# Pairing the quarter products of dK and dV in a cached-attention backward kernel

## The chip, the core and the metric

The kernel runs on one core of one Trainium2 chip. The metric is the device time of one execution in microseconds (us). Three executions before the change took 1729.28, 1730.04 and 1733.95 us, so the median is 1730.04 us. A separate execution was profiled; its own time is given with the profile below.

## The reference

The program computes one decoder block for two sequences with one new token each, and the gradient of every input. The block is a layer norm modulated by a conditioning vector, attention of 32 heads over a cache of 8192 keys and values per head, and a gated feed-forward layer. The parts that carry the memory traffic are these:

```python
k_cache, v_cache : (2, 32, 8192, 128) bf16        # B, H, Sk, Dh
scores = einsum('bhqd,bhkd->bhqk', q, k_cache) * 128 ** -0.5
p      = softmax(scores)
o      = einsum('bhqk,bhkd->bhqd', p, v_cache)    # then @ wo, residual, layer norm, SwiGLU
_out, _vjp = jax.vjp(f, A_x, A_k_cache, A_v_cache, A_wq, A_wo, B_w1, B_w3, B_w2, c, w_mod)
return (_out, *_vjp(grad_out))
```

There is one query per head, so the gradients of the two caches are outer products. For one head, with p the softmax weights, do the gradient of o, and dp = v_cache · do: dV[k, :] = p[k] · do, and dK[k, :] = p[k] · (dp[k] − Σ p·dp) · q · 128 ** -0.5. Each of dK and dV is as large as a cache, 2 MB per head. The program therefore reads K once and V up to twice, and writes dK and dV once, for 2 × 32 = 64 heads.

## The kernel before, in words

**Tiling.** A head's 8192 keys are spread over 128 partitions, 64 keys each (`KK`). All large tiles are halves of a head: 128 partitions by 32 keys by 128 values in bf16, 1 MB, 8 KB per partition. They come from one pool of 21 buffers called `half` (`NHALF`). K halves, V halves, the output halves of dK and dV, the large weights and some other things all use this pool.

**Jobs.** A head has two jobs. Job A (lines 390 to 572, `job_a`) is the forward part: it loads K and V, transposes K on TensorE in 8 groups (`a_t`), forms the scores, the maximum, the exponentials, scales K by the exponentials in four quarter products on VectorE (`a_scale`, L468), and contracts with V (`a_m`, L483). Job C (lines 1133 to 1239) is the backward part: it loads V again, transposes it in 8 groups (`c_t`), forms dp (`c_s`, or `c_rows` and `c_cols` for the heads in the set `crow`), turns that into ds (`c_ds`, L1212), and writes dV and dK. Before job C's first slot, `c_spread` puts the two row vectors of the head, called `DOr` (for dV) and `Qr` (for dK), on all partitions.

**Quarter products.** `outer` (L1184) makes one quarter of dV or dK: one VectorE product of 128 x 2048 elements (L1191), half of a half tile. It takes a new `half` buffer when the quarter is the first of its half tile, and issues the 1 MB store to memory from GpSimd's queue (L1196) when the quarter is the second. Six slots after the store, the planner counts the buffer as free (`back`) and lets loads that are due go out (`pump`).

**Order.** The whole order of work is written out by hand, as a list of slots. `at(slot, place, f)` puts a piece of work in a slot, and `place` sets the order within a slot: transposes (`PL_T`) come before the maximum (`PL_MAX`), then the K scaling and dV products (`PL_TT`), then ds (`PL_DS`), then dK products (`PL_DK`), then other tasks. Every engine executes its instructions in the order that this list gives. Loads are issued from SyncE's queue in the order of their due slot, as early as the count of free buffers lets `pump` issue them. The real waits on buffers are semaphores.

**Stages.** A job occupies 8 slots of transposes (`NG`) and further slots for what follows. From the code's arithmetic, slots 0 to 319 hold 40 jobs A, one every 8 slots. From slot 320 to 703, 24 jobs A and 24 jobs C alternate, each pair taking 16 slots, with job C on the first 8. From slot 704 on there are 40 jobs C alone, one every 8 slots; the second sequence's feed-forward chain and what leads to its attention gradient are laid beside them in slots 721 to 777. The last job C starts at slot 1016, which the code calls `max(sC)`. Heads 25 to 31 and the last two heads (62 and 63) are not in `crow`; all others are.

**Where the products lie before.** With job C starting at slot s, the four dV quarters (`c_dv`) lie at s, s+2, s+4 and s+6. The four dK quarters (`c_dk`) lie at s+11, s+13, s+15, s+17, or one slot later for heads in `crow`. The ds they need is made at s+10, or s+11 in `crow`.

Of the kernel before, what the change touches and what calls it, by code (L numbers as in the profile page):

```python
# [17 lines left out]
def kernel(  # L18
# [44 lines left out]
    NG = KK // GRP  # L63
    NQ = KK // QK
    LAG = 2
# [119 lines left out]
    def load_v(key, i, hf):  # L185
        t = htile()
        qd.dma_start(t[:], src_of(A_v_cache, i)[:, hf * HK:(hf + 1) * HK, :])
        free["half"] -= 1
        V[(key, hf)] = t
# [138 lines left out]
    def at(slot, place, f):  # L328
        seq[0] += 1
        events.setdefault(slot, []).append((place, seq[0], f))  # L330

    now = [0]
    PL_EXP, PL_T, PL_X, PL_S, PL_B, PL_MAX, PL_TT, PL_M, PL_FREE, PL_EV, PL_DS, PL_DK, PL_TASK = range(13)
# [4 lines left out]
    def want(need, f):  # L338
        seq[0] += 1
        loads.append((need, seq[0], f))  # L340
# [725 lines left out]
    sC = []  # L1066
    s = NG * H
# [10 lines left out]
    s = max(s, TC)  # L1078
# [12 lines left out]
    s = max(s, t1 + 5)  # L1091
# [41 lines left out]
    def c_t(n, g):  # L1133
        if g == 0:
            if n in crow:
                b, h = hb(n)
                nc.gpsimd.tensor_copy(qz[2 + n % 2][:, NSL - 1:NSL], DO_bf[:, b, h:h + 1])
            else:
                DP[n] = head_ps()
        spare = A_END <= now[0] < t1 or now[0] >= max(sC) - 5 * NG  # L1140
        kts[("c", n, g)] = transposes(lambda j: vb_(("c", n), g * GRP + j), g in (2, 6) and not spare)
        if g % HG == HG - 1:
            V.pop((("c", n), g // HG))
            release()
            pump()

    crow = {n for n in range(NHD) if R0 < sC[n] < A_END - NG or t1 < sC[n]}
# [6 lines left out]
    def c_rows(n):  # L1154
        kts[("crow", n)] = rows_out(("c", n))

    def c_cols(n):
        DP[n] = head_ps()
        cols_out(DP[n], kts.pop(("crow", n)))

    def c_s(n, g):
        if n in crow:
            return s_rows(("c", n), n, g, c_bank)
        b, h = hb(n)
        kt = kts.pop(("c", n, g))
        for j in range(GRP):
            cc = g * GRP + j
            nc.tensor.matmul(DP[n][:, cc:cc + 1], kt[:, j, :], DO_bf[:, b, h:h + 1], start=True, stop=True)  # L1168

    def c_spread(n):  # L1170
        b, h = hb(n)
        ps = scr(2 * P) if R0 <= now[0] <= A_END else mtps()[:, 0:2 * P]
        nc.tensor.matmul(ps[:, 0:P], Qr_bf[:, b, h:h + 1].to_broadcast((P, P)), identb[:], start=True, stop=True)
        nc.tensor.matmul(ps[:, P:2 * P], DOr_bf[:, b, h:h + 1].to_broadcast((P, P)), identb[:],
                         start=True, stop=True)
        for k, (nm, bufs) in enumerate((("Qr", 3), ("DOr", 2))):
            t = hw.tile([P, P], BF16, name=nm, tag=nm, bufs=bufs)
            nc.scalar.copy(t[:], ps[:, k * P:(k + 1) * P])
            QD[(n, k)] = t
        e = hw.tile([P, KK, 2], BF16, name="e2", tag="e2", bufs=3)  # L1180
        nc.scalar.copy(e[:], E["t"][:, n % E["n"], :].unsqueeze(2).to_broadcast((P, KK, 2)))
        E2[("c", n)] = e

    def outer(store, dst, n, which, w2, q):  # L1184
        hf, o = divmod(q * QK, HK)
        if o == 0:
            free["half"] -= 1
            store[(n, hf)] = htile()
        t = store[(n, hf)]
        ks = slice(q * QK, (q + 1) * QK)  # L1190
        nc.vector.tensor_tensor(  # L1191
            pair(t[:, o:o + QK, :]),
            QD[(n, which)][:].rearrange("p (a b) -> p a b", b=2).unsqueeze(1).to_broadcast((P, QK, P // 2, 2)),
            w2[:, ks, :].unsqueeze(2).to_broadcast((P, QK, P // 2, 2)), ALU.mult)
        if o + QK == HK:
            sq_.dma_start(src_of(dst, n)[:, hf * HK:(hf + 1) * HK, :], t[:])  # L1196
            store.pop((n, hf))

            def back():
                release()  # L1200
                pump()

            at(now[0] + 6, PL_FREE, back)

    def c_dv(n, q):
        outer(dvt, out_3, n, 1, E2[("c", n)], q)
        if q == NQ - 1:
            QD.pop((n, 1))

    def c_ds(n):  # L1210
        t = hw.tile([P, KK, 2], BF16, name="ds2", tag="ds2", bufs=2)
        nc.vector.scalar_tensor_tensor(t[:], DP.pop(n)[:, 0:KK].unsqueeze(2).to_broadcast((P, KK, 2)),  # L1212
                                       SIG_f[:, n:n + 1], E2.pop(("c", n))[:], ALU.subtract, ALU.mult)
        ds2[n] = t

    def c_dk(n, q):
        outer(dkt, out_2, n, 0, ds2[n], q)
        if q == NQ - 1:
            ds2.pop(n)
            QD.pop((n, 0))  # L1220

    for n in range(NHD):
        s = sC[n]
        for g in range(NG):
            at(s + g, PL_T, lambda n=n, g=g: c_t(n, g))
            at(s + g + LAG, PL_S, lambda n=n, g=g: c_s(n, g))
        at(s - 3, PL_B, lambda n=n: c_spread(n))
        for q in range(NQ):
            at(s + 2 * q, PL_TT, lambda n=n, q=q: c_dv(n, q))
            at(s + NG + LAG + 1 + (n in crow) + 2 * q, PL_DK, lambda n=n, q=q: c_dk(n, q))  # L1230
        x = 1 if n in crow else 0
        if x:
            at(s + NG + LAG, PL_EXP, lambda n=n: c_rows(n))
            at(s + NG + LAG + 1, PL_EXP, lambda n=n: c_cols(n))
        at(s + NG + LAG + x, PL_DS, lambda n=n: c_ds(n))

        for hf in range(2):
            if n not in kept:
                want(s + hf * HG, lambda n=n, hf=hf: load_v(("c", n), n, hf))
# [304 lines left out]
```

## Time and profile before

| Quantity | Value |
|---|---|
| Median of three executions | 1730.04 us |
| Profiled execution, its own time | 1731.2 us |
| Profiled execution, span from first to last instruction | 1729.4 us |
| TensorE matmul busy | 1447.8 us, 84% |
| VectorE (DVE) busy | 1149.6 us, 66% |
| ScalarE (ACT) busy | 1046.1 us, 60% |
| GpSimd (POOL) busy | 344.9 us, 20% |
| Bytes moved | 708.92 MB, mean 410 GB/s |
| Loads on SyncE's queue (q1) | 421.59 MB |
| Stores on GpSimd's queue (q0) | 268.45 MB |
| Granted TensorE clock, mean | 0.828 |

The profile calls the queue of a DMA by the engine that issues it: SP for loads, POOL for stores of dK and dV, ACT for small outputs. The DMA share in a window is the mean busy share of the core's 16 DMA engines; it is summed from packet durations and reads 1.01 when all of them are busy without a gap. A "half" in a row's name is a buffer of the shared pool.

### The profile page before, as it was taken

To read this page: it belongs to the slowest core of one execution; us is meant where nothing else is said; L and a number is where in the kernel's file an instruction comes from. 1 tells how busy PE (TensorE), PEld (TensorE's weight loads), DVE (VectorE), ACT (ScalarE), POOL (GpSimd) and SP (SyncE) were. 2 spreads that over 40 slices of the span, in tenths; PEclk is the share of its full clock that TensorE was granted. 3 is DMA by queue.
4 is the path that set the end of the run, shared out by engine and by line. 5 is a ranking of instruction groups with operands and counts; after the bars stand their busy time and mean duration, and the time that the engine had idled before them with its cause. 6 is when DMAs were issued, how large, how long until landed. Compare 5 with 4: busy or idle time off the path is not lost.

```text
span 1729.4 us, 48571 instructions
## 1 busy us (share of the span) xinstructions
PE 1447.8 (84%) x20883; PEld 1155.6 (67%) x20883; DVE 1149.6 (66%) x1575; ACT 1046.1 (60%) x1536; POOL 344.9 (20%) x726
## 2 busy tenths in 40 slices
PE   5999999989988878887788888975599997797962
PEld 5999998879776666665666666875355565455551
DVE  2666666867877677666667766785586675666554
ACT  4666666646565556555555555697576676566772
POOL 0333333322211111111111112111121111111111
PEclk7999999988999898898888998698765567556586
DMA  9999999999999999999999998999999999999997
GB/s 382 418 418 419 418 419 388 419 387 390 379 412 424 425 425 420 424 418 418 420 419 418 424 419 358 397 416 420 426 411 419 413 410 419 423 420 420 417 420 303
DMA packets 109379, 708.92 MB, mean 410 GB/s; under 512 B 11175, under 2 KB 17683, under 8 KB 27243
## 3 DMA queue, kind: packets, MB, share of 16 engines
q1 hardware_dynamic: 67280, 421.59, 59.4%
q0 software_dynamic: 36864, 268.45, 37.4%
q10 hardware_dynamic: 5019, 15.78, 2.3%
q8 instruction: 163, 2.67, 0.6%
q14 instruction: 53, 0.43, 0.1%
HBM read 421.57 MB, written 284.20 MB: 408 GB/s over the span
## 4 chain that ended last, share of the span: by engine, by line
DMA 45%; PE 35%; DVE 6%; ACT 6%; issue 5%; SPq 1%; POOL 0%; ACTq 0%; POOLq 0%; DVEq 0%
DMA out_dram<-half 24%; DMA half<-in_A_k_cache_dram 16%; PE tp L380 14%; PE m_ps L483 8%; DVE half L1191 4%; DMA out_dram<-stg 3%; ACT kt L385 3%; PE s_ps L442 2%; PE k_ps L505 2%; PE s_ps L433 2%; PE m_ps L413 1%; DMA half<-in_w_mod_dram 1%; PE m_ps L1323 1%; DVE ek L468 1%; PE k_ps L413 1%
## 5 line engine op out<-in xcount | busy, mean ns | idle before, releaser
L385 ACT COPY kt<-tp 128x1024 bf16<-128x1024 bf16 x794 | 796.6, 1017 | 560.0 <-PE tp L380 511.4
L380 PE MATMUL tp<-identb,half 128*128 128x128 bf16 x8192 | 725.3, 243 | 85.8 <-DMA half<-in_A_k_cache_dram 51.2
L380 PEld LDWEIGHTS <-half 128*128 128x128 bf16 x8192 | 579.7, 110 | 212.5 <-issue 149.0
L383 DVE COPY kt<-tp 128x1024 bf16<-128x1024 bf16 x230 | 158.6, 690 | 294.0 <-PE tp L380 291.5
L483 PE MATMUL m_ps<-ek,half 128*128 128x129 bf16 x4096 | 335.6, 225 | 6.9 <-DVE ek L468 3.8
L1196 POOL DMA_DIRECT2D out_dram<-half x256 | 136.2, 532 | 895.2 <-DVE half L1191 734.6
L483 PEld LDWEIGHTS <-half 128*128 128x128 bf16 x4096 | 257.3, 100 | 28.0 <-issue 27.7
L433 PE MATMUL s_ps<-ssel,srow 128*128 128x16 f32 x640 | 98.6, 288 | 49.6 <-ACT srow L420 49.2
L433 PEld LDWEIGHTS s_ps<-ssel,srow 128*128 128x128 f32 x640 | 91.8, 221 | 63.7 <-ACT srow L420 63.4
L442 PE MATMUL s_ps<-qT_bf,kt 128*128 128x1 bf16 x2496 | 107.4, 164 | 0.8 <-DVE lnst L1030 0.4
L442 PEld LDWEIGHTS <-kt 128*128 128x128 bf16 x2496 | 96.6, 97 | 1.3 <-issue 1.0
L1324 ACT CAST stg<-m_ps 128x512 bf16<-128x512 f32 (+2 forms) x124 | 72.8, 588 | 36.0 <-DMA out_dram<-stg 17.6
L1323 PE MATMUL m_ps<-half 2*128 2x512 bf16 (+2 forms) x124 | 70.1, 565 | 12.4 <-DVE d_h_312 L1436 7.3
L505 PE MATMUL k_ps<-half,pz 128*32 128x512 bf16 x1024 | 68.7, 389 | 3.4 <-POOL pz L491 3.2
L454 DVE TENSOR_REDUCE nm<-s_ps 128x1 f32<-128x128 f32 x64 | 18.7, 291 | 36.0 <-PE s_ps L451 35.9
L1168 PE MATMUL s_ps<-DO_bf,kt 128*128 128x1 bf16 x576 | 25.6, 165 | 18.6 <-DVE kt L383 14.5
L505 PEld LDWEIGHTS <-pz 128*32 128x32 bf16 x1024 | 21.6, 97 | 25.1 <-POOL pz L491 5.6
L1168 PEld LDWEIGHTS <-kt 128*128 128x128 bf16 x576 | 24.4, 101 | 19.8 <-DVE kt L383 14.6
L1323 PEld LDWEIGHTS <-half 2*128 2x128 bf16 (+1 forms) x124 | 12.7, 102 | 34.3 <-issue 31.7
L413 PE MATMUL k_ps<-kt,qz_110 128*32 128x512 bf16 x240 | 32.9, 525 | 1.0 <-ACT kt L385 1.0
L413 PE MATMUL k_ps<-kt,qz_109 128*32 128x512 bf16 x240 | 33.3, 535 | 0.0
L1298 ACT CAST half<-m_ps 2x512 bf16<-2x512 f32 (+1 forms) x36 | 20.2, 565 | 20.0 <-PE m_ps L1295 19.4
(899 smaller groups left out, 1996.3 us busy)
## 6 DMA issues: line engine op xcount, KB each, us to landing
out_dram<-half POOLq DMA_DIRECT2D x256, 1024.0 KB, 17.9
half<-in_A_v_cache_dram SPq DMA_DIRECT2D x252, 1024.0 KB, 14.3
half<-in_A_k_cache_dram SPq DMA_DIRECT2D x128, 1024.0 KB, 19.6
out_dram<-stg ACTq DMA_DIRECT2D x22, 512.0 KB, 11.5
half<-in_A_wq_dram SPq DMA_DIRECT2D x8, 1024.0 KB, 13.0
half<-in_A_wo_dram SPq DMA_DIRECT2D x4, 1024.0 KB, 21.6
half<-in_w_mod_dram SPq DMA_DIRECT2D x3, 1024.0 KB, 10.9
half<-in_B_w_dram SPq DMA_DIRECT2D x3, 1024.0 KB
```

What stands on the lines that cost most here:

```text
L380: nc.tensor.transpose(tp[:, j, :], block(j), identb[:])
L383: nc.vector.tensor_copy(kt[:], tp[:])
L385: nc.scalar.copy(kt[:], tp[:])
L413: nc.tensor.matmul(R_ps[key][NR * j:NR * (j + 1), :], w, kt[:, o:o + SW, :], start=(a == 0), stop=(a == NSL - 1))
L433: nc.tensor.matmul(sv[:, c, :], t[:, c * P:(c + 1) * P], ssel[:], start=True, stop=True)
L442: nc.tensor.matmul(S_ps[i][:, cc:cc + 1], kt[:, j, :], qT_bf[:, h, b:b + 1], start=True, stop=True)
L483: nc.tensor.matmul(m[:, 0:P + 1], vb_(i, kk), t[:, kk % QK, 0:P + 1], start=(kk == 0), stop=(kk == KK - 1), skip_group_check=True)
L505: nc.tensor.matmul(kp["ps"][NR * j:NR * (j + 1), :], pz[:, o:o + NR], K[(i, kk // HK)][:, kk % HK:kk % HK + QP, :], start=False, stop=(h = ...
L1191: nc.vector.tensor_tensor(pair(t[:, o:o + QK, :]), QD[(n, which)][:].rearrange("p (a b) -> p a b", b=2).unsqueeze(1).to_broadcast((P, QK, ...
L1196: sq_.dma_start(src_of(dst, n)[:, hf * HK:(hf + 1) * HK, :], t[:])
L1323: nc.tensor.matmul(ps[:lw, 0:rw], rsl(ln, lc, lw, step), rsl(rn, rc, rw), start=True, stop=True)
L1324: nc.scalar.copy(st["t"][:lw, o:o + rw], ps[:lw, 0:rw])
```

## The change

The change moves the quarter products to other slots. Nothing else in the program is edited, and no operation is added or removed. The numbers are: `NG` = 8, `LAG` = 2, `NQ` = 4.

```diff
@@ for n in range(NHD): s = sC[n]
         for q in range(NQ):
-            at(s + 2 * q, PL_TT, lambda n=n, q=q: c_dv(n, q))
-            at(s + NG + LAG + 1 + (n in crow) + 2 * q, PL_DK, lambda n=n, q=q: c_dk(n, q))
+            x, y = 2 + q + q // 2 * 2, NG + LAG + 2 + q + (q // 2 * 2 if s < max(sC) else 0)
+            at(s + x, PL_TT, lambda n=n, q=q: c_dv(n, q))
+            at(s + y, PL_DK, lambda n=n, q=q: c_dk(n, q))
```

The dV quarters now lie at s+2, s+3, s+6 and s+7: the two quarters of one half tile are in neighbouring slots. The dK quarters lie at s+12, s+13, s+16 and s+17 for all heads, in `crow` or not. In the last job they lie at s+12, s+13, s+14 and s+15. The `half` buffer is still taken at the first quarter of a half tile and the store is still issued at the second, so these two now lie one slot apart where they were two slots apart.

## The prediction, made before the changed kernel was run

> **What bounds the kernel now.** I read four views, from coarse to fine. First, the page's 40 slices.
>
> ```profile
> DVE  2666666867877677666667766785586675666554
> DMA  9999999999999999999999998999999999999997
> GB/s 382 418 418 419 418 419 388 419 387 390 379 412 424 425 425 420 424 418 418 420 419 418 424 419 358 397 416 420 426 411 419 413 410 419 423 420 420 417 420 303
> ```
>
> The DMA engines are busy in every slice but slice 25 and the last one. No compute engine comes near that. The change touches only work from slot 320 on, so I asked for windows by stage (columns: window, length, busy time of each engine with its count, granted clock, DMA share, GB/s).
>
> ```profile
> 270.00:480.00 210.00, 196.60 (x3843) 177.80 (x3840) 151.33 (x289) 121.72 (x178) 56.70 (x107) 0.94 0.99 391
> 480.00:1060.00 580.00, 478.21 (x6248) 374.13 (x6248) 402.44 (x479) 323.07 (x491) 101.19 (x276) 0.90 1.01 421
> 1060.00:1095.00 35.00, 28.38 (x480) 24.13 (x477) 29.34 (x36) 19.56 (x32) 8.74 (x16) 0.80 0.84 323
> 1095.00:1712.00 617.00, 492.30 (x5126) 345.58 (x5123) 408.72 (x519) 420.39 (x615) 92.28 (x183) 0.67 1.01 418
> 1712.00:1729.00 17.00, 0.00 (x0) 0.00 (x0) 0.00 (x0) 0.00 (x0) 0.00 (x0) 0.50 0.30 128
> ```
>
> The alternating stage (480 to 1060) and the stage of jobs C alone (1095 to 1712) run with all 16 DMA engines full. The one hole inside the changed part is 1060 to 1095. It lacks (1.01 − 0.84) × 35 = 6 us of DMA work. The last 17 us is the drain: compute ended at about 1706, and the engines finish one after another.
>
> Third, the waits. The first row is GpSimd's store queue, the others SyncE's load queue and VectorE.
>
> ```profile
> POOL out_dram L1196 <- DVE half L1191: 734.6, 161, 20.8
> SPq L187 <- DMA out_dram<-half: 772.6, 100, 21.7
> SPq L181 <- DMA out_dram<-half: 194.6, 45, 5.0
> DVE half L1191 <- DMA out_dram<-half: 111.4, 30, 16.7
> ```
>
> A store waits for its product, a load waits for a store to give its buffer back, and a product may wait for a buffer too. This is a closed loop through the DMA engines. It stays full as long as some issued bytes are still under way. To see the cover, I subtracted from the bytes issued the bytes whose packets had ended, every 0.5 us, from the trace's DMA records (in MB of 1,048,576 bytes). In the alternating stage the mean is about 3 MB and the lowest point of most 40 us stretches lies between 1.2 and 2 MB, 3 us at 0.42 MB per us. In the stage of jobs C alone, from 1140, the mean is mostly 3 to 6 MB with low points of 1.4 MB near 1143 and 1.26 MB near 1253 and else above 2.4 MB. At 1068 it is 0.07 MB: that is the hole.
>
> Fourth, VectorE's order of time at the hole.
>
> ```profile
> 1057.72 1.23 DVE L1191 TENSOR_TENSOR half<-Qr,ds_20501 128x2048 bf16<-128x2048 bf16 x1 [2.40 <-DMA out_dram<-half]
> 1058.86 0.68 DVE L383 COPY kt<-tp 128x1024 bf16<-128x1024 bf16 x1
> 1059.46 1.22 DVE L1191 TENSOR_TENSOR half<-Qr,ds_20501 128x2048 bf16<-128x2048 bf16 x1
> 1060.59 1.22 DVE L1191 TENSOR_TENSOR half<-DOr,e_20552 128x2048 bf16<-128x2048 bf16 x1
> 1064.78 1.22 DVE L1191 TENSOR_TENSOR half<-Qr,ds_20501 128x2048 bf16<-128x2048 bf16 x1 [2.97 <-PE tp L380]
> 1065.93 0.68 DVE L383 COPY kt<-tp 128x1024 bf16<-128x1024 bf16 x1
> 1066.53 1.22 DVE L1191 TENSOR_TENSOR half<-DOr,e_20552 128x2048 bf16<-128x2048 bf16 x1
> 1067.66 1.22 DVE L1191 TENSOR_TENSOR half<-Qr,ds_20501 128x2048 bf16<-128x2048 bf16 x1
> 1068.79 0.22 DVE L446 TENSOR_REDUCE rm<-s_ps 128x1 bf16<-128x64 f32 x1
> ```
>
> Two half tiles are being filled at once here, dK of head 23 (`Qr`) and dV of head 24 (`DOr`). The second half of dK waits until 1064.78 for a buffer that the transposes still read. Its store goes out at 1068.04 and the one of dV at 1069.17, while the DMA engines starve.
>
> **What the Trainium skill says.** "DMA: Bandwidth & Descriptors", section "Issuing engines are not separate DMA queues": transfers from all issuing engines share the same 16 DMA engines. The trace agrees: loads from SP and stores from POOL together give a share of 1.01. Its section "Where 436 GB/s comes from" puts the ceiling at 435 GB/s; the trace holds 421. So nothing is to be had from moving stores about while the share is 1.01. "VectorE: DVE Perf Modes", section "The perf-mode tier table", gives 1224 ns for a bf16 product of 2048 elements; the trace has 1215 to 1225. "SBUF — State Buffer", section "Who interferes with whom": a VectorE instruction with two SBUF inputs contends with a GpSimd instruction that reads SBUF. The trace is compatible: GpSimd's copy at L470 took 1.08 us beside a product at 1070.04, and 0.24 at 1045.26.
>
> **The change part by part.** It removes and adds nothing: 512 products of 1.22 us and 256 stores of 0.53 us on POOL stay. No edit is costed by a new instruction; what counts is where each store lands and what stands behind it.
>
> *Alternating stage, 24 pairs.* In slots after s (mod 16), stores move from 14, 2, 2, 6 to 13, 1 (dK) and 3, 7 (dV). Their order on VectorE, by the places in a slot, becomes: scale, dK0, dK1, kt copy, dK2, dK3, kt copy, dV0, rm, dV1, nm, kt copy, scale, dV2, dV3, scale. I lay this on the cycle at 924 to 946 and the one before. dK1 falls into the 1.15 us that VectorE waits ahead of the kt copy at 929.13, so its store leaves at about 929 in place of 931.25. dK3 follows the kt copy at 932.0 or so, its store about 4 us ahead of 936.39. dV1 now stands behind dV0 and rm, about 1 us later than 935.26. dV3 stands behind one more product in its slot: 921.0 becomes about 922.1. Sum: −2.2 − 4.2 + 1 + 1.1, so the mean store is 1 us earlier. Behind dV2 and dV3 stands the second `a_scale` product, 1.13 us (the start-to-start step) later; the TensorE product L483 waits for it. VectorE has 1.78 us of idle before the next copy in that cycle (923.63), which takes this up, and TensorE waited for L468 only 3.8 us in the whole stage. All this is hidden by the DMA backlog. The thinnest point is just before the dV3 store; 1.2 to 1.4 MB is 3.0 to 3.5 us, the store is 1.1 us later. Cost 0. Without the cover it would cost 24 × 1.1 = 26 us.
>
> *Jobs C alone.* In `crow` heads, two buffers used to be asked for in the same slot (dV0 with dK2, dV2 with dK0), and both stores of a slot pair came together. Now a half begins every second slot and a store leaves every second slot. A buffer is held one slot less: 7 counted slots in place of 8 for each of four halves in 8 slots, so 3.5 in place of 4 are out on average. That is half a buffer more for loads. The 108.7 us that VectorE waits for stores in this stage may shrink. With the share at 1.01, the gain is 0.
>
> *The hole at 1060 to 1095.* With the new slots, dK of head 23 lies at 700, 701, 704, 705 and dV of head 24 begins at 706. dK1 follows dK0 at once, its store about 0.7 us earlier than 1060.97. dK2 comes ahead of dV0 and gets the buffer that dV0 got at 1060.59. dK3 follows, and the store leaves at about 1063.2 in place of 1068.04. dV0 inherits the wait to 1064.78, behind the kt copy: 1065.4 to 1066.6. Then comes rm, at 1066.6 in place of 1068.79. TensorE waits 2.81 us for this rm with its matmul L451, and all of its later transposes stand behind that, as does the load issued at 1073.95, which waits for transposes. So the chain through the hole is 2.2 us shorter. I take −2.2; bounds are 0 (the buffers come free in another order and the hole only moves) and −5.4 (all of it filled).
>
> *Heads 25 to 31 and the start.* dV stores are one slot later (about 1.5 us) and the dK ones are not earlier, while the backlog from 1095 to 1112 falls to 1.0 MB. The first dV store of all (466.15) is one slot later behind a hole at 456 to 468. I take +0.2 in all, bounds 0 and +3.
>
> *The tail.* The last dK quarters lie in consecutive slots, last store at slot 1031 in place of 1034. VectorE already makes them back to back (four in 4.63 us from 1701.46). Their stores then wait for earlier stores, as these two lines show.
>
> ```profile
> 1705.36 0.53 POOL L1196 DMA_DIRECT2D out_dram<-half  x1 [1.93 <-DMA out_dram<-half]
> 1707.81 0.53 POOL L1196 DMA_DIRECT2D out_dram<-half  x1 [1.93 <-DMA out_dram<-half]
> ```
>
> Gain 0: what is left in flight, about 3 MB at 1700, ends when it ends. The spread of the 16 engines at the end (from about 1712 to 1726) can shift by some us with any change of order; I allow ±4.
>
> Sum: 1731.2 (profiled execution: span 1729.4 and 1.8 around it) − 2.2 + 0.2 = 1729.2. The median of the runs is 1.2 below the profiled one, so 1728.0.
>
> **The rivals.** (1) *The hole closes and more.* Stores are evenly spaced, so the next thin spots (0.26 MB at 1086, 1.0 at 1111) fill as well: −5.4 for the hole and up to −2 at the drain, 1730 − 7 = 1723. For it: VectorE's wait at 1061.8 is a result of two open halves. Against it: while the hole lasts, DVE is 29.3 of 35 us busy, so the work there can't shrink much. (2) *The loop starves* in the alternating stage: dV3's store, and the loads that wait for it, come later than the cover. It decides once the store is more than 3 us late at the thinnest point. At 0.4 us of starvation per pair, 24 × 0.4 = +10, 1740. For it: loads in that stage waited 317.8 us for stores. Against it: three of four stores are earlier or within 1 us. (3) *The products are not paired in time*, because VectorE's queue is full and the waits set the order: nothing moves, 1730.
>
> **How the numbers follow.** About 0.3%, 5.2 us, is what this measurement can tell from no change. Small move from the hole, 1728: 0.45. Nothing, 1730: 0.15. Rival 1: 0.20, mostly beyond 0.3%. Rival 2: 0.20. So faster 0.20, same 0.60, slower 0.20. The likeliest cases' own range is 1724 to 1733. The range takes in the hole's bound, 1730 − 5.4 − 4 = 1721 (rounded), and most of rival 2, to 1738.
>
> **What would show it.** The alternating stage and jobs C keep a DMA share of 1.01. Two products of one half run back to back in their rows, and POOL's stores leave about every 3.8 us in the last stage. The share from 1060 to 1095 rises from 0.84 to about 0.9. TensorE's wait for rm of 2.81 us goes. I am wrong if a window between 480 and 1712 other than the hole falls below 0.97, if SP's wait for stores moves to transposes or products, or if the drain grows past 20 us.

## The result and the profile after

The changed kernel takes 1770.41 us (median of 4 runs, 1770.21 to 1772.47), beside 1731.99 us for the kernel before in the same comparison (1729.28 to 1734.5). The ratio is 1.0225, with a 95% interval from 1.0204 to 1.0245: slower, by 38.4 us in the medians. The forecast was 1728.0 us, with a range from 1721 to 1738. The profiled execution took 1770.21 us, its span is 1768.4 us.

The page's slices of the changed kernel show where the time went.

```profile
DVE  2666666858666566576676666778386665657564
DMA  9999999999999999999999999999999999999997
GB/s 383 419 419 418 418 418 389 419 381 393 377 397 398 390 374 408 397 374 406 380 401 407 387 393 381 364 403 421 426 421 420 417 410 418 423 421 418 421 420 305
```

Before, slices 12 to 24 moved 412 to 425 GB/s. Now the same slices, the alternating stage, move 374 to 408. Slices 25 to 27 hold the end of that stage and the change to the next (364 to 403); from slice 28 to slice 39 the rate is back at 410 to 426. The DMA row alone would hide this: it still reads 9 everywhere. The same in windows by stage (columns as before, the last three being granted clock, DMA share and GB/s):

```profile
480.00:1080.00 600.00, 478.89 (x6029) 377.46 (x6027) 392.86 (x463) 315.67 (x476) 108.45 (x268) 0.87 0.99 395
...
1170.00:1752.00 582.00, 476.48 (x4539) 324.62 (x4536) 388.07 (x456) 396.69 (x583) 86.42 (x176) 0.65 1.01 419
1752.00:1768.00 16.00, 0.00 (x0) 0.00 (x0) 0.00 (x0) 0.00 (x0) 0.00 (x0) 0.50 0.26 110
```

The last stage (419 GB/s, before 418) and the drain are as before. The loss lies in the alternating stage. Between the first dV products of successive heads there were 24.95 us on average before, and there are 26.69 now. Over the 23 such steps that makes 23 × 1.74 = 40 us, which covers the whole loss of 38.4 us.

VectorE's waits from 470 to 1060 name what is new (columns: total us, times, longest). First the kernel before, then the changed one.

```profile
DVE kt L383 <- PE tp L380: 128.7, 59, 7.4
...
DVE half L1191 <- DMA out_dram<-half: 2.4, 1, 2.4
```

```profile
DVE half L1191 <- DMA out_dram<-half: 93.4, 22, 5.9
DVE kt L383 <- PE tp L380: 77.1, 50, 3.9
```

In 22 of about 23 steps VectorE now stands still for some 4 us, until a store to memory has read out the buffer that the next product is to write. Before, only one product of this stage waited so. TensorE then waits for VectorE's copies, and the K loads, behind it all, wait for TensorE. In the same window of the kernel before, TensorE's longest wait was for the K loads themselves:

```profile
PE tp L380 <- DMA half<-in_A_k_cache_dram: 49.8, 29, 4.9
```

These are TensorE's and SyncE's rows of the changed kernel:

```profile
PE tp L380 <- DVE kt L383: 63.0, 25, 4.4
```

```profile
SPq L181 <- DMA out_dram<-half: 84.8, 22, 8.5
SPq L181 <- PE m_ps L483: 54.6, 19, 3.5
```

The chain of waits of the changed kernel, followed back in a window of two steps, closes on itself (columns: start us, us, what).

```profile
902.61 10.60 DMA out_dram<-half
...
913.30 0.13 DVE half L1191
...
925.46 0.14 DVE ek L468
925.61 0.99 issue
926.60 2.37 DVE half L1191 x2
928.96 0.29 issue
929.25 9.82 DMA out_dram<-half
```

The store at 902.61 lands at 913.2. The product at 913.30 is the first dK quarter of one head. The work after it leads to the last two dV quarters of the next head at 926.60, and to their store at 929.25, which the next first dK quarter waits for again. One turn takes 929.25 − 902.61 = 26.6 us. The DMA engines need 24.95 us for the 10 MB of a turn, so the loop, and no longer the DMA engines, sets the pace.

**Which buffer is taken.** The built programs say which of the 21 `half` buffers each tile gets. In the alternating stage the buffers are given out in about the order in which they were last used. I counted what the buffer of the first half tile of dK held before:

| | kernel before | changed kernel |
|---|---|---|
| first half of dK takes a buffer that V held | 23 of 24 | 0 |
| first half of dK takes a buffer that a store still reads | 1 of 24 | 23 of 24 |
| K loads that wait for a store (trace, 470 to 1060) | 45, 194.6 us | 22, 84.8 us |

The first two rows are counts from the programs; VectorE's waits above, one product before and 22 now, agree with them.

The reason is in the planner's count of free buffers, which `back` does six slots after a store. The last dV store was in slot s+6, its count came at s+12, and the place of the count, `PL_FREE`, stands ahead of `PL_DK` in a slot. So a K load took the oldest free buffer, the one of that store, and waited for it in SyncE's queue, where such waits did not hold the rate below 421 GB/s. Then dK's first quarter, at s+12 too, took the next buffer, which V had left long before. With the store in slot s+7, the count comes at s+13, behind the dK quarter at s+12. The dK quarter takes the oldest buffer, and it is VectorE that waits for the store.

### The profile page after: what moved, and what is told of

It reads as the page before. It is cut to its first block, busy times and chain, and to the rows that moved or that the text cites. A ratio compares the mean times of both kernels' runs of the same rounds, so it can differ in the third digit from the quotient of the medians.

```text
span 1768.4 us, 48520 instructions
## 1 busy us (share of the span) xinstructions
PE 1481.4 (84%) x20883; PEld 1183.1 (67%) x20883; DVE 1154.1 (65%) x1575; ACT 1049.2 (59%) x1536; POOL 350.7 (20%) x726
## 4 chain that ended last, share of the span: by engine, by line
DMA 41%; PE 30%; DVE 12%; issue 11%; ACT 4%; POOL 1%; SPq 1%; DVEq 0%; POOLq 0%; ACTq 0%
DMA out_dram<-half 32%; PE tp L380 13%; DVE half L1191 8%; DMA half<-in_A_k_cache_dram 7%; PE m_ps L483 7%; PE s_ps L433 3%; PE s_ps L442 2%; ACT kt L385 2%; PE k_ps L505 2%; PE m_ps L413 2%; DMA half<-in_w_mod_dram 1%; DVE kt L383 1%; DVE ek L468 1%; ACT srow L420 1%; DMA half<-in_A_wo_dram 1%
## 5 line engine op out<-in xcount | busy, mean ns | idle before, releaser
L385 ACT COPY kt<-tp 128x1024 bf16<-128x1024 bf16 x794 | 799.0, 1017 | 603.0 <-PE tp L380 559.8
L380 PE MATMUL tp<-identb,half 128*128 128x128 bf16 x8192 | 745.3, 246 | 94.3 <-DVE kt L383 91.9
L380 PEld LDWEIGHTS <-half 128*128 128x128 bf16 x8192 | 597.9, 112 | 217.0 <-issue 214.1
L483 PE MATMUL m_ps<-ek,half 128*128 128x129 bf16 x4096 | 328.4, 222 | 12.6 <-DVE ek L468 8.7
L483 PEld LDWEIGHTS <-half 128*128 128x128 bf16 x4096 | 250.3, 98 | 33.5 <-issue 32.4
L433 PE MATMUL s_ps<-ssel,srow 128*128 128x16 f32 x640 | 116.5, 318 | 32.8 <-ACT srow L420 31.2
L433 PEld LDWEIGHTS s_ps<-ssel,srow 128*128 128x128 f32 x640 | 109.6, 258 | 47.6 <-ACT srow L420 47.3
L442 PEld LDWEIGHTS <-kt 128*128 128x128 bf16 x2496 | 96.9, 97 | 1.4 <-issue 1.0
L1411 ACT COPY kt<-tp 128x1024 bf16<-128x1024 bf16 x28 | 29.5, 1052 | 9.1 <-PE tp L1405 7.7
L413 PEld LDWEIGHTS <-qz_109 128*32 128x32 bf16 x448 | 12.8, 98 | 31.8 <-issue 13.6
```

Source lines behind the costliest of these rows:

```text
L380: nc.tensor.transpose(tp[:, j, :], block(j), identb[:])
L385: nc.scalar.copy(kt[:], tp[:])
L413: nc.tensor.matmul(R_ps[key][NR * j:NR * (j + 1), :], w, kt[:, o:o + SW, :], start=(a == 0), stop=(a == NSL - 1))
L433: nc.tensor.matmul(sv[:, c, :], t[:, c * P:(c + 1) * P], ssel[:], start=True, stop=True)
L442: nc.tensor.matmul(S_ps[i][:, cc:cc + 1], kt[:, j, :], qT_bf[:, h, b:b + 1], start=True, stop=True)
L483: nc.tensor.matmul(m[:, 0:P + 1], vb_(i, kk), t[:, kk % QK, 0:P + 1], start=(kk == 0), stop=(kk == KK - 1), skip_group_check=True)
```

## The experiments

Two theories stand against each other. Theory 1: the exchange of buffers between the K load and dK closes a loop. Theory 2: the places of the products starve the DMA engines (the prediction's rival 2). The times below are medians, the ratios are to the kernel before, with 95% intervals.

**The changed kernel with an earlier count.**

```diff
-            at(now[0] + 6, PL_FREE, back)
+            at(now[0] + 5, PL_FREE, back)
```

> The changed kernel with one number different: the planner counts a stored half's buffer as free 5 slots after its store instead of 6, so the count comes at s+12 again for the second half of dV, ahead of dK's first quarter in that slot, and the K load rather than dK takes that buffer (23 of 24 dK first halves then take a buffer that V held, as before the change; in the changed kernel 23 of 24 take one that a store still reads). Theory 1 (the buffer hand-over makes VectorE wait for a store) expects 1726 to 1734 us and VectorE's wait for stores in the alternating stage back from 93 us to under 10 us. Theory 2 (the places of the products themselves, dV's second store one slot later and a K scaling behind two products, starve the DMA engines) expects 1765 to 1772 us, unchanged.

1731.74 us beside 1732.86, ratio 0.9999 (0.9989 to 1.0008). The whole loss is gone with every product in its new slot. VectorE's waits for stores are no longer among its six longest in that stage, and the first half of dK takes a buffer of V in 23 of 24 cases. Its window in the alternating stage, again at full rate:

```profile
480.00:1040.00 560.00, 458.23 (x6059) 359.95 (x6059) 395.73 (x464) 315.28 (x479) 100.85 (x269) 0.91 1.01 421
```

So theory 2 falls as the cause of this loss.

**The kernel before with a later count.** Its products stay in their old slots.

```diff
-            at(now[0] + 6, PL_FREE, back)
+            at(now[0] + 7, PL_FREE, back)
```

> The kernel before, its products where they were, with the buffer counted as free 7 slots after the store instead of 6: the count for dV's second half comes at s+13, behind dK's first quarter at s+12, and 23 of 24 dK first halves take the buffer that dV's store still reads. Theory 1 expects the loss without any product having moved: 1760 to 1772 us, with some 90 us of VectorE waiting for stores in the alternating stage. Theory 2 expects 1728 to 1734 us, as before.

1739.14 us, ratio 1.004 (1.0023 to 1.0057). Slower without any product moved, but by 6 us only; both expectations missed. The waits are all there:

```profile
DVE half L1191 <- DMA out_dram<-half: 97.3, 23, 6.2
```

VectorE waits as long as in the changed kernel (93.4 us), yet most of the time is not lost. So the wait alone is not the price: what counts is the length of the loop that it closes. I took the loop apart in each trace: from the end of the instruction that issues the last dV store to the start of the first dK product, and from there to the next such store (medians).

| kernel | store to dK | dK to next store | sum | measured step (mean) | ratio |
|---|---|---|---|---|---|
| old slots, count at 7 | 10.68 us | 14.77 us | 25.45 us | 25.45 us | 1.0040 |
| dV moved only | 10.62 us | 15.80 us | 26.42 us | 26.11 us | 1.0146 |
| dV at 2, 3, 5, 6, count at 7 | 10.56 us | 15.82 us | 26.38 us | 26.18 us | 1.0111 |
| changed kernel | 10.12 us | 16.84 us | 26.96 us | 26.69 us | 1.0225 |
| kernel before | no loop | no loop | | 24.95 us | 1 |

The landing of a store costs all four the same 10 to 11 us. With the old slots the loop is 25.45 us, just above the 24.95 us of the DMA engines. The new slots make the second part 2 us longer, and that is where the loss gets its size. The steps don't add up to the times exactly: 23 of them come to 12, 27, 28 and 40 us more than before, in the order of the table, and the medians are 6, 24, 18 and 38 us longer. Where the rest is regained was not traced.

The length of the second part also goes with TensorE's granted clock. These are two such stretches of the changed kernel, from the first dK product to the next last dV store, and the same eight matmuls of each, from the chain:

```profile
673.07:686.59 13.52, 11.72 (x162) 8.81 (x159) 12.81 (x15) 10.67 (x19) 2.91 (x6) 1.00 1.00 391
913.30:929.25 15.95, 12.04 (x128) 9.20 (x125) 13.00 (x15) 9.53 (x15) 2.92 (x7) 0.79 1.01 423
```

```profile
678.37 1.06 PE s_ps L433 x8
...
918.57 1.89 PE s_ps L433 x8
```

In the trace's clock records of the changed kernel, 6.9 us of an average second part ran at half of the full clock. In the kernel with the old slots and the count at 7 it was 7.1 us, so the clock does not explain the difference between these two. But in the three turns of the changed kernel without any half clock the second part, counted as in the table, took 14.0 to 14.1 us in place of the median of 16.84. With the store's 10.12 us, an estimate for a turn at full clock is some 24.2 us, less than the 24.95 us of the DMA engines. So the size of the loss may depend on the clock too; no run here changed the clock alone.

**dV alone and dK alone.** Each keeps one of the two changed lines; the other line is the old one.

```diff
 dV moved only:
-            at(s + y, PL_DK, lambda n=n, q=q: c_dk(n, q))
+            at(s + NG + LAG + 1 + (n in crow) + 2 * q, PL_DK, lambda n=n, q=q: c_dk(n, q))
 dK moved only:
-            at(s + x, PL_TT, lambda n=n, q=q: c_dv(n, q))
+            at(s + 2 * q, PL_TT, lambda n=n, q=q: c_dv(n, q))
```

> Only the dV quarters are moved (s+2, s+3, s+6, s+7); dK stays at s+11 or s+12 and every second slot. The count for dV's second half comes at s+13, behind dK's first quarter. Theory 1 expects 1755 to 1775 us, nearly the whole loss. Theory 2 expects a loss too, as dV's second store is the late one, so this run does not tell them apart alone; both say slow.

> Only the dK quarters are moved (s+12, s+13, s+16, s+17); dV stays at s, s+2, s+4, s+6, so that its buffer count comes at s+12, ahead of dK's first quarter. Theory 1 expects 1726 to 1734 us. A third theory, that pairing dK's quarters in itself holds up the dV products and the copies on VectorE, expects part of the loss here: 1740 to 1760 us.

dV alone: 1757.07 us, ratio 1.0146 (1.013 to 1.0162), at the low end of what was expected. dK alone: 1732.5 us, ratio 0.9996 (0.9987 to 1.0005), no loss. So the dV line brings the exchange of buffers. Pairing dK costs nothing by itself. Once the loop is closed, the second part is 16.84 − 15.80 = 1.04 us longer with it, but the first part is 0.50 us shorter, and the measured step grows by 26.69 − 26.11 = 0.58 us. Over 23 steps that is 13 us, the distance of the two times.

**The last stage alone.** The new slots only for the jobs C from slot 704 on.

```diff
-            at(s + x, PL_TT, lambda n=n, q=q: c_dv(n, q))
-            at(s + y, PL_DK, lambda n=n, q=q: c_dk(n, q))
+            at(s + (x if s >= 704 else 2 * q), PL_TT, lambda n=n, q=q: c_dv(n, q))
+            at(s + (y if s >= 704 else NG + LAG + 1 + (n in crow) + 2 * q), PL_DK, lambda n=n, q=q: c_dk(n, q))
```

> The new slots only for the 40 jobs C from slot 704 on; the 24 alternating ones keep the old slots. Theory 1 puts the loss into the loop of the alternating stage (a store of dV, its landing, the first dK product that takes its buffer, and the work up to the next such store: 26.7 us per pair in the changed kernel against 24.95 us before, over 23 pairs = 40 us) and expects 1729 to 1735 us here, with a DMA share of 1.01 in the last stage, although more products take stored buffers there. A theory that the last stage loses too expects 1737 us or more.

1731.24 us, ratio 1.0 (0.9987 to 1.0012), DMA share 1.01 and 419 GB/s from 1200 to 1700. The last stage neither gains nor loses, although VectorE waits for a store 49 times from 1130 on (124.8 us), in place of 28 times (108.7 us) in the kernel before.

**Later dK.** The changed kernel, with the first dK pair behind the count.

```diff
-            x, y = 2 + q + q // 2 * 2, NG + LAG + 2 + q + (q // 2 * 2 if s < max(sC) else 0)
+            x, y = 2 + q + q // 2 * 2, NG + LAG + 2 + q + (q < 2) + (q // 2 * 2 if s < max(sC) else 0)
```

> The changed kernel with dK's first two quarters one slot later (s+13 and s+14). The buffer count of dV's second half at s+13 stands ahead of dK in the slot, so the K load takes that buffer again. Theory 1 expects 1728 to 1735 us and no wait of VectorE for stores in the alternating stage, though dK comes later than in the changed kernel. If lateness of products were the cause, it would be 1770 us or more.

1734.11 us, ratio 1.0013 (1.0004 to 1.0022). Moving the products still later takes the loss away, but for about 2 us that I didn't trace further. The count of the last dV store stays at s+13 here, as late as in the changed kernel. So a late count alone is not the cause either; what matters is whether it comes before or after dK's first quarter.

**The same slots with and without the exchange.** dV's second pair one slot earlier, at s+5 and s+6. In one kernel the count stays at 6, in the other it is 7.

```diff
-            x, y = 2 + q + q // 2 * 2, NG + LAG + 2 + q + (q // 2 * 2 if s < max(sC) else 0)
+            x, y = 2 + q + q // 2, NG + LAG + 2 + q + (q // 2 * 2 if s < max(sC) else 0)
 and in the second kernel also (its dV slots are written (2, 3, 5, 6)[q], which is the same):
-            at(now[0] + 6, PL_FREE, back)
+            at(now[0] + 7, PL_FREE, back)
```

> The changed kernel with dV's second pair one slot earlier (s+5 and s+6), so the store is at s+6 and its buffer count at s+12, ahead of dK's first quarter. Theory 1 expects 1728 to 1735 us and under 10 us of VectorE waiting for stores in the alternating stage.

> The same slots as the run before this one (dV at s+2, s+3, s+5, s+6, dK in pairs), but the buffer counted as free 7 slots after the store, so that 23 of 24 dK first halves take the buffer of the dV store again. Every product stands where it stands in that run; only the buffers differ. Theory 1 expects the loop to close: some 10.5 us from the dV store's issue to dK's first product, and 15.5 to 16.5 us from there to the next such store, so 26 to 27 us per pair and 1755 to 1772 us in all. If the slots alone decided, it would be equal to the run before it.

1730.07 us, ratio 0.9986 (0.9979 to 0.9994), against 1750.4 us, ratio 1.0111 (1.009 to 1.0132). Every product stands in the same slot in both; only the time at which the planner counts a buffer, and with it who takes which buffer, differs. The loads keep their order as well, and SyncE's queue holds nothing but loads, so the count can act through the buffers alone. That is worth 20 us. The second kernel falls short of the 1755 us expected, at the measured 26.18 us per turn. Its window and its wait:

```profile
480.00:1040.00 560.00, 467.31 (x5722) 366.63 (x5721) 373.47 (x438) 300.45 (x454) 106.28 (x255) 0.84 1.00 402
```

```profile
DVE half L1191 <- DMA out_dram<-half: 94.5, 22, 5.5
```

The first of the two is the only kernel here with an interval below 1, by 0.14%. It is less than the 0.3% named in the prediction, so I claim no gain for it.

## Why the prediction was wrong, point by point

- **What bounds the kernel: right before, not after.** The DMA engines did bound the alternating stage, and the last stage stays so. The closed loop through buffers was described in the prediction ("a product may wait for a buffer too"), but as something that the backlog covers as a whole. I never asked how long one turn of it is.
- **The alternating stage, "Cost 0": the step that failed.** I listed where each store moves in time and what stands behind it on VectorE, and compared a lateness of 1.1 us with a cover of 3 us. I took the buffers as a mere count ("A buffer is held one slot less", in the part on jobs C alone). What the later store moved as well was its count, from s+12 to s+13, past dK's first quarter in s+12. That changed who takes which buffer. The lines that bore on it were at hand: in the kernel before, SyncE waited for stores 194.6 us with its K loads, and VectorE waited 2.4 us in this stage. The question to ask was what would exchange these two. It was not asked. The runs show in its place a closed turn of 26.69 us where the DMA engines need 24.95. The cover was no fixed amount either: from 490 to 1050, the bytes issued and not yet moved, counted as in the prediction, were 3.2 MB on average and never below 1.18 before; in the changed kernel they are 2.2 MB on average and fall to 0.18.
- **The store times.** I expected the first two stores of a turn 2 and 4 us earlier. That was worked out without the new wait of 4 us at the first dK quarter, which stands ahead of both.
- **Jobs C alone, gain 0: right.** The run with the new slots only there shows 1.0.
- **The hole at 1060 to 1095, −2.2 us: wrong.** With the loop broken again (count at 5), TensorE's wait of 2.81 us for the row maximum is gone, as said, but the share from 1060 to 1095 is 0.86, against 0.84 before, and the time differs by no more than −1.9 to +1.4 us by its interval. So most of the hole is not set by that wait. What else sets it wasn't tried. The prediction's sizes for the hole also differ: its share gives 6 us, its bound for all of it is 5.4, and by rate (323 in place of 421 GB/s over 35 us) it is 8 us.
- **The tail, gain 0: right.** The drain is about as long, 16 us against 17.
- **Rival 2** named the right stage and the right sign and was given 0.20. Its mechanism, a store more than 3 us late at the thinnest backlog, isn't what happened, and its price of 0.4 us per pair was too small: it is 1.74 us. Its evidence counted only the V loads' waits for stores (317.8 us); the K loads' 194.6 us, the waits that changed places, were left out. The range ended at 1738 and missed by 32 us.
- **My own signs.** "A window falls below 0.97" would not have caught this: the share in the alternating stage is 0.99. SyncE's waits did move to TensorE's work, as the second sign said.
- **A smaller reading.** The products of the kernel before took 1211 to 1260 ns, 93% of them within the 1215 to 1225 that the prediction gives. Nothing rests on it.

## What to carry to other kernels

When a shared pool of buffers feeds engines that work in order, moving a product or a store also moves the moment at which its buffer is handed on. Check who takes that buffer next: here the load queue waited for stores for 194.6 us with the DMA engines still full, while VectorE, which works in order, held up the copies that TensorE needed. Then add up one whole turn of the loop that such a wait closes, from store to landing to product to next store, and compare it with the time that the bounding resource needs per turn; the wait total alone doesn't tell the loss (97 us of waiting cost 6 us in one kernel, and 93 us cost 38 in another).

## What was unexpected in the hardware's numbers

The DMA share hardly shows a shortage of work. In the alternating stage (490 to 1050 us), the rate fell from 420.7 to 394.0 GB/s, 6%, while the share fell from 1.011 to 0.993. The packets took longer: loads of 8 KB 333.6 ns on average in place of 314.4, and 7.4% of them over 400 ns in place of 1.5%. With the count at 5 they are back at 313.8 ns and 1.2%. The long ones don't start when little is under way: in the changed kernel 13% of those that started with over 3 MB issued and not yet moved took over 400 ns, and 0.4% of those that started with under 1 MB. Why they are longer is open. The rate in GB/s is the better gauge there.
